# A new timetable for one core: the same 2,473 steps of a gated linear attention and an FFN, ordered anew

## The chip, the cores and the metric

One core of a Trainium2 chip runs the whole kernel. Its engines each take their own instructions in the order in which the program issues them: TensorE (PE, with the weight loads in a row of their own, PEld), VectorE (DVE), ScalarE (ACT), GpSimd (POOL), and SyncE (SP), which here only issues transfers. The metric is device time of one execution in microseconds (us); less is better.

## The reference

Two parts, one after the other. First a recurrence over 768 steps for 4 batches x 8 heads with 48 x 48 states:

```python
cur = einsum('bhd,bhe->bhde', u * k[t], v[t])
y[t] = einsum('bhd,bhde->bhe', r[t], state + cur)
state = w[t][..., None] * state + einsum('bhd,bhe->bhde', k[t], v[t])
```

Then an FFN on its output, seen as x of 3,072 tokens x 384 (8 heads x 48): `h = max(x @ w_in, 0)`, `out = (h * h) @ w_out`, with 2,048 hidden columns. `w_in` and `w_out` are 64-bit floats, everything else 32-bit. Output: 3,072 x 384 in 32 bit.

## The kernel before

**Tiling.** Time is cut into 6 chunks of 128 steps; a chunk of one batch is a unit, so there are 24 units. A chunk's four units make 512 tokens, for which the FFN runs in 16 slices of 128 hidden columns. Each slice (line 827, `ffn`) is one *first product* `hp` (9 matmuls, line 852), then `g1` (ReLU, ACT), `g2` (square; ACT in chunk 0, else DVE), `g3` (the upper part, ACT), `g4` (the rest, DVE, line 864), then four *second products* `ob`, one per batch (3 matmuls of 128 x 384 each, line 870), which add up in four PSUM banks `obs`. Products are made of upper and lower parts, which is why there are three matmuls where one would do. Six slices of chunk 0 and all 16 of chunk 1 run in two halves of two batches. Steps carry a number as their name: `hp 0` to `hp 5` are slices 0 to 5 for batches 0 and 1 of chunk 0, `hp 6` to `hp 11` the same for batches 2 and 3, `hp 12`, `hp 14`, ... the full slices, and `hp 32` is the first of chunk 1.

**Attention of a unit in chunk 0.** w, k and r arrive in time-major form and PE turns them (`turn`, line 496); DVE scans the products of w (`scan`, line 508); ACT takes logarithm and exponential (`ln`, `exp`) and copies r (`rc`, line 518); DVE multiplies (`rk` line 523, `rt`, `kn`, `kn2`, `kq`); PE makes `bp`, `mt` (scores), `mix`, `mix2` and `dS` (the new state); ACT and DVE write x as upper part and rest (`x`, line 584, `xl`, line 587). From chunk 1 on the turning is done by two DVE transposes (`z`, line 460) and 16 small transfers from SBUF to SBUF (`pt`, line 470), and PE's part is `ktp`, `dS`, `mt`, `past` and `mix` in chunk 1, `ktp` and one joint `mix` later. The state of a batch is updated by POOL (`SE`, line 680), which waits for PE's use of the old state. x of two batches is completed by small transfers (`send`, line 705).

**Weights.** Eight groups of two slices. A group g comes by five transfers for w_in (one of 384 KB, four of 96 KB; line 398) and one of 768 KB for w_out (line 400), still in 64 bit; `split_w` makes two 32-bit parts of each by ACT, three DVE steps (lines 415, 419, 424), ACT and a POOL subtraction (line 432). w, k and r come as 192 KB per batch (line 451; for two batches at once 384 KB), v as four transfers of 48 KB per unit (line 483).

**What sets the order.** All work is first recorded as 2,473 steps (`Plan.add`, with an engine, what is read and written, and buffers), numbered as they are added. `Plan.run` then issues them in the order of the table `ORDER`, takes each buffer's place from `PLACES`, and puts ahead of some PE steps the fillers that `FILLS` lists: step: (count, pool, place). A filler is a transpose of the identity into an unused place (`fill`, line 334); 16 of them run at the very start in any case. As every engine takes its instructions in order of issue, the table is the order of six queues: 593 steps on PE, 658 on ACT, 729 on DVE, 65 on POOL, 423 transfers on SP and 5 on ACT's queue. Semaphores are set from the reads and writes, whatever the order.

**Steps that the texts name by number**: 373, 380, 387, 401, 415 are `hp 0`, `hp 1`, `hp 2`, `hp 4`, `hp 6`; 781 and 788 are the first two first products of chunk 1.

Of the kernel before, what the change touches and what calls it, by code (L numbers as in the profile page):

```python
# [96 lines left out]
class Names:  # L97
# [122 lines left out]
def kernel(  # L220
# [12 lines left out]
    V, A, G, T = nc.vector, nc.scalar, nc.gpsimd, nc.tensor  # L233
# [3 lines left out]
    C = 128  # L237
# [777 lines left out]
```

## Time and profile before

| | us |
|---|---|
| median of 3 runs | 532.66 (532.25 to 536.98) |
| the profiled execution, span | 533.0 |
| PE busy | 515.3 (97%) |
| PEld, DVE, ACT, POOL busy | 464.7, 358.4, 312.6, 77.6 |
| first products, line 852: 1,062 matmuls | 220.9 busy |
| second products, line 870: 1,152 matmuls | 228.1 busy |

A busy time is the union of an engine's instructions, so it says where an engine had something in hand, not that it was of use: a filler counts as busy. The profile has 5,478 PE matmuls, which is every one of the program, so each PE step can be found in the timeline by counting. 53.07 MB pass the transfer queues in 222,982 packets, 212,672 of them under 512 bytes.

### The profile page before, as it was taken

How to read it: one execution, taken by the hardware profiler on the slowest of the kernel's cores; microseconds unless marked ns; L12 is line 12 of the kernel's file. 1: busy time of each engine (PE TensorE's matmuls, PEld its weight loads, DVE VectorE, ACT ScalarE, POOL GpSimd, SP SyncE). 2: the span in 40 equal slices, each digit the busy share in tenths (PEclk: the TensorE clock that was granted, in tenths of full speed). 3: DMA queues.
4: the chain of work that ended last, by engine and by line, in shares of the span. 5: the costliest groups of instructions: out<-in, count | busy, mean ns of one | idle time of the engine just before them, and what ended most of it. 6: DMA issues, size and time to landing. Idle time of an engine off the chain costs nothing.

```text
span 533.0 us, 13849 instructions
## 1 busy us (share of the span) xinstructions
PE 515.3 (97%) x5478; PEld 464.7 (87%) x5478; DVE 358.4 (67%) x782; ACT 312.6 (59%) x858; POOL 77.6 (15%) x117
## 2 busy tenths in 40 slices
PE   8998999999999999899999999999999999999996
PEld 8787998778899989788998988898998898989995
DVE  4899887887768799766877768648366654333332
ACT  2778888777675667757557384655345554432322
POOL 2012441242403030030300300201200000000000
PEclk9999999999999999999999999999999999999999
DMA  9999869946465655636555363543450010200001
GB/s 144 168 241 218 179 148 204 236 81 119 85 129 121 117 117 109 124 77 129 107 92 110 61 134 73 100 77 80 89 117 1 5 31 17 71 6 1 0 1 63
DMA packets 222982, 53.07 MB, mean 100 GB/s; under 512 B 212672, under 2 KB 217792, under 8 KB 222912
## 3 DMA queue, kind: packets, MB, share of 16 engines
q1 hardware_dynamic: 222192, 51.15, 48.1%
q8 instruction: 45, 0.74, 0.6%
q10 hardware_dynamic: 720, 0.98, 0.6%
q14 instruction: 25, 0.20, 0.1%
HBM read 31.65 MB, written 4.72 MB: 68 GB/s over the span
## 4 chain that ended last, share of the span: by engine, by line
PE 69%; SPq 3%; DVE 2%; DMA 2%; issue 0%; ACT 0%; POOL 0%; ACTq 0%; DVEq 0%; POOLq 0%
PE ob L870 31%; PE hp L852 30%; SPq L470 2%; PE ob L644 2%; PE ob L663 2%; PE a L653 2%; PE a L626 1%; PE hp L608 1%; DMA x<-x 1%; DVE st L460 0%; DMA pt<-st 0%; DMA v<-in_v_dram 0%; SPq L483 0%; PE hp L548 0%; DVE pt L508 0%
## 5 line engine op out<-in xcount | busy, mean ns | idle before, releaser
L870 PE MATMUL ob<-wo,g 128*128 128x384 f32 x1152 | 228.1, 341 | 2.1 <-ACT x L584 2.1
L852 PE MATMUL hp<-x,wi 128*128 128x512 f32 (+1 forms) x1062 | 220.9, 354 | 1.5 <-DVE g L864 1.3
L870 PEld LDWEIGHTS ob<-wo,g 128*128 128x128 f32 x1152 | 199.6, 188 | 9.6 <-ACT x L584 2.3
L852 PEld LDWEIGHTS hp<-x,wi 128*128 128x128 f32 x1062 | 174.6, 189 | 27.7 <-DVE g L864 4.0
L857 ACT ACTIVATE t<-hp 128x512 f32<-128x512 f32 (+1 forms) x118 | 61.0, 517 | 89.1 <-PE hp L852 53.5
L861 DVE SCALAR_TENSOR_TENSOR hp<-hp,t 128x512 f32<-128x512 f32 (+1 forms) x96 | 58.1, 605 | 78.3 <-ACT t L857 78.1
L864 DVE TENSOR_TENSOR g<-hp,g 128x512 fp32r<-128x512 f32 (+1 forms) x118 | 69.1, 586 | 39.9 <-ACT g L863 38.4
L863 ACT CAST g<-hp 128x512 fp32r<-128x512 f32 (+1 forms) x118 | 59.5, 507 | 47.0 <-DVE hp L861 46.2
L603 ACT ACTIVATE m<-diag,beta 128x64 f32<-128x64 f32 x160 | 40.3, 339 | 0.0
L508 DVE TENSOR_TENSOR_SCAN pt<-pt,zero 112x128 f32<-112x128 f32 x80 | 30.8, 420 | 7.3 <-DMA pt<-st 4.1
L634 POOL MEMSET S<- 1x1 f32 x16 | 1.4, 88 | 193.1 <-PE ob L644 192.5
L584 ACT ACTIVATE x<-ob 112x128 fp32r<-112x128 f32 x64 | 15.7, 277 | 21.0 <-PE ob L663 13.6
L557 POOL TENSOR_TENSOR st<-st 128x384 f32<-128x384 f32 x16 | 16.6, 1035 | 78.3 <-DVE st L460 53.2
L460 DVE STREAM_TRANSPOSE st<-st 128x1152 f32<-128x1152 f32 x20 | 26.9, 1360 | 0.2 <-DMA st<-in_w_dram 0.2
L587 DVE SCALAR_TENSOR_TENSOR x<-ob,x 112x128 fp32r<-112x128 f32 x64 | 16.6, 282 | 13.1 <-ACT x L584 9.3
L432 POOL TENSOR_TENSOR wi<-q,wi 128x768 fp32r<-128x768 f32 x8 | 16.2, 2026 | 50.1 <-ACT wi L431 46.5
L515 ACT ACTIVATE m<-pt 112x512 f32<-112x512 f32 x24 | 15.2, 632 | 9.0 <-DVE pt L508 8.8
L531 DVE TENSOR_TENSOR pt<-pt,m 112x512 f32<-112x512 f32 x24 | 17.2, 716 | 4.3 <-ACT Ec L530 1.9
L801 ACT COPY ob<-zero 112x128 f32<-112x128 f32 x64 | 16.3, 271 | 4.8 <-DVE x L587 3.2
L432 POOL TENSOR_TENSOR wo<-q,wo 128x768 fp32r<-128x768 f32 x8 | 14.8, 1856 | 25.0 <-ACT wo L431 22.7
L610 ACT COPY m<-hp 128x448 f32<-128x448 f32 (+1 forms) x20 | 9.9, 494 | 13.5 <-PE hp L608 13.2
L685 DVE COPY_PREDICATED m<-caus,a 128x256 f32<-128x256 uint8 x40 | 16.9, 439 | 1.1 <-PE a L653 1.0
(127 smaller groups left out, 540.1 us busy)
## 6 DMA issues: line engine op xcount, KB each, us to landing
pt<-st SPq DMA_DIRECT2D x120, 96.0 KB, 2.3
ro<-in_moe_w_out_dram SPq DMA_DIRECT2D x8, 768.0 KB, 6.6
v<-in_v_dram SPq DMA_DIRECT2D x96, 48.0 KB, 2.5
st<-in_r_dram SPq DMA_DIRECT2D x11, 384.0 KB, 5.1
st<-in_w_dram SPq DMA_DIRECT2D x11, 384.0 KB, 5.2
st<-in_k_dram SPq DMA_DIRECT2D x11, 384.0 KB, 4.6
out_dram<-q SPq DMA_DIRECT2D x20, 192.0 KB, 2.2
ri<-in_moe_w_in_dram SPq DMA_DIRECT2D x8, 384.0 KB, 5.2
```

The source lines that it names most:

```text
L432: P.add("pool", 1.9, rank(8 * k + 5), lambda q=q, tt=tt: G.tensor_tensor(out=tt[:, 1], in0=q.tile, in1=tt[:, 0].bitcast(F32), op=ALU.subtr ...
L460: V.transpose(out=zt[:, i].rearrange("a t p q i -> a t (p q) i"), in_=sv[:, :, i].rearrange("s t p q x -> s t (p q) x"))
L508: lambda p=p: V.tensor_tensor_scan(out=pt[:, 0, p], data0=src(0)[:, p], data1=zero.broadcast_to([HP, C]), initial=1.0, op0=ALU.mult, op1=A ...
L531: P.add("dve", 0.6, rank("kn"), lambda: V.tensor_tensor(out=pt[:, 0], in0=pt[:, 0], in1=yv(), op=ALU.mult), r=[y0], w=EK, port=True)
L603: A.activation(M.tile[:, o:o + Q], diag2, AF.Copy, scale=beta.tile[:, i:i + 1])
L685: P.add("dve", 0.36, rank("mask"), lambda j=j: V.copy_predicated(out=mv(j), mask=caus[:, :, 0:Q].unsqueeze(1).broadcast_to([128, 2, 2, Q]) ...
L852: T.matmul(hp.tile[:, 0:n], wi[f][:, wl, kt], xT[:, kt, xl, xs], start=(m == 0), stop=(m == 3 * KT - 1))
L857: P.add("act", 0.49 if full else 0.28, rank("g1"), lambda: A.activation(t(), h(), AF.Relu), r=[hp], w=[(g, 1)])
L861: P.add("dve", 0.605 if full else 0.337, rank("g2"), lambda: V.scalar_tensor_tensor(out=h(), in0=h(), scalar=0.0, in1=t(), op0=ALU.max, op ...
L863: P.add("act", 0.48 if full else 0.26, rank("g3"), lambda: A.copy(out=hi(), in_=h()), r=[hp], w=[(g, 0)])
L864: P.add("dve", 0.605 if full else 0.335, rank("g4"), lambda: V.tensor_tensor(out=lo(), in0=h(), in1=hi().bitcast(F32), op=ALU.subtract), r ...
L870: T.matmul(obs[b][:, 0:DM], g.tile[0][:, gl, o:o + C], wo[f][:, wl], start=(f == 0 and m == 0), stop=(f == NF - 1 and m == 2))
```

## The change

`ORDER`, `PLACES` and `FILLS` are replaced; the steps and their instructions are the same. One function changes: in `clear`, which records the four steps `zero` ahead of the joint mixes, each step now names as its predecessors the steps of chunk 0 that use the same bank of `obs`. This narrows the orders that a table may have; it adds no instruction.

```diff
 ORDER = (
-    0, 4, 11, 6, 94, 1, 14, 18, 5, 19, 20, 17, 10, 21, 8, 9, 139, 15, 7, 16, 12, 23, 2, 13, 24, 22, 25, 92, 26, 30, 27, 101,
...
+    10, 5, 0, 4, 14, 178, 18, 19, 54, 6, 1, 2, 17, 20, 26, 16, 23, 21, 15, 24, 51, 25, 22, 7, 55, 58, 9, 12, 30, 31, 33, 57, 64, 27, 60, 28, 29, 59, 11, 61,
...
 FILLS = {
-    443: (2, 'a', 1), 571: (3, 'a', 0), 363: (3, 'a', 0), 370: (4, 'hp', 1), 578: (5, 'hp', 1), 493: (3, 'hp', 0), 645: (2, 'side', 0), 511: (6, 'side', 0),
-    520: (2, 'side', 0), 634: (5, 'side', 0), 663: (4, 'hp', 0), 1215: (1, 'hp', 1), 15: (29, 'ob', 1), 30: (8, 'ob', 3), 39: (6, 'ob', 0), 80: (6, 'ob', 2),
-    89: (5, 'hp', 0), 142: (3, 'hp', 0), 124: (12, 'ob', 0), 133: (11, 'ob', 0), 162: (6, 'ob', 0),
+    14: (20, 'ob', 0), 16: (7, 'ob', 1), 55: (4, 'ob', 3), 56: (10, 'ob', 1), 71: (14, 'ob', 0), 99: (2, 'ob', 0), 41: (3, 'ob', 1), 48: (16, 'ob', 1),
+    101: (2, 'ob', 1), 82: (3, 'hp', 0), 89: (11, 'ob', 1), 156: (16, 'ob', 0), 165: (12, 'side', 0),
 }
...
     def clear(rank):
         for p in range(NP):
+            turned = [s for s in P.steps if s.name.endswith(f" of chunk 0, batch {s.name[-1]}") and ("ob", p) in s.keys]
-            P.add("act", 0.16, rank("zero"), lambda p=p: A.copy(out=obs[p][0:HP, DM:], in_=zero[0:HP].broadcast_to([HP, C])), w=[("YO", p)], banks=1 << p)
+            P.add("act", 0.16, rank("zero"), lambda p=p: A.copy(out=obs[p][0:HP, DM:], in_=zero[0:HP].broadcast_to([HP, C])), w=[("YO", p)], after=turned, banks=1 << p)
```

Read with the steps' names, PE's queue begins like this (c0b2: chunk 0, batch 2; a number in brackets: so many fillers ahead of the step):

```
before: ut, turn c0b0, [29] turn c0b0, turn c0b0, [8] bp c0b0, turn c0b2, turn c0b1, turn c0b1, turn c0b1, mt c0b0, [6] mix c0b0,
 turn c0b2, bp c0b1, mix2 c0b0, mt c0b1, turn c0b3, dS c0b0, [6] mix c0b1, mix2 c0b1, turn c0b2, [5] dS c0b1, [3] turn c0b3, hp 0,
 bp c0b2, turn c0b3, hp 1, bp c0b3, mt c0b2, [12] mix c0b2, mix2 c0b2, [11] dS c0b2, [6] mt c0b3, ob 0, hp 2, hp 3, mix c0b3, ob 0, ob 1, ...
after: [20] turn c0b0, ut, [7] turn c0b0, turn c0b0, [4] turn c0b1, bp c0b0, turn c0b1, [10] turn c0b1, [14] bp c0b1, mt c0b0,
 [2] turn c0b2, turn c0b3, mt c0b1, mix c0b0, [3] mix2 c0b0, turn c0b2, [16] dS c0b0, [2] turn c0b2, mix c0b1, [3] mix2 c0b1, bp c0b2,
 [11] dS c0b1, hp 0, turn c0b3, hp 1, turn c0b3, [16] bp c0b3, mt c0b2, hp 2, mix c0b2, ob 0, mix2 c0b2, ob 0, hp 3, ob 1, ...
```

and in chunk 1's attention, from its 72nd step on, like this:

```
before: hp 16, [3] bp c1b1, ob 12, ob 12, bp c1b0, hp 18, [3] ktp c1b0, ob 12, ob 12, dS c1b0, [4] mt c1b0, [5] past c1b0, ob 14, mix c1b0, ...
after: hp 16, bp c1b0, ob 12, ob 14, ob 12, ob 12, hp 18, ob 14, ob 14, ob 12, ktp c1b0, ob 16, ob 16, bp c1b1, dS c1b0, ob 16, ob 14, mt c1b0, ...
```

SP's queue begins before with w, a quarter of v, r (batch 0), r (batches 2 and 3), k (batch 0); after with a quarter of v, k, w (batch 0), 96 KB of weights 0, a quarter of v (batch 1), r (batch 0).

## Rows read from the trace of the kernel before

**Rows 1.** The page: busy time by engine, clock by slice, one costly group.
```profile
PE 515.3 (97%) x5478; PEld 464.7 (87%) x5478; DVE 358.4 (67%) x782; ACT 312.6 (59%) x858; POOL 77.6 (15%) x117
...
PEclk9999999999999999999999999999999999999999
...
L801 ACT COPY ob<-zero 112x128 f32<-112x128 f32 x64 | 16.3, 271 | 4.8 <-DVE x L587 3.2
```

**Rows 2.** Windows by stage: us, busy us (count) by engine, clock, DMA share, GB/s.
```profile
0.00:33.00 33.00, 28.98 (x361) 25.72 (x362) 22.99 (x62) 17.70 (x52) 4.40 (x21) 1.00 1.01 173
33.00:60.99 27.99, 25.79 (x342) 23.32 (x340) 25.94 (x42) 23.04 (x64) 7.86 (x5) 1.00 0.89 213
60.99:140.00 79.01, 75.53 (x770) 65.58 (x771) 66.27 (x113) 64.01 (x156) 26.19 (x17) 1.00 0.73 152
140.00:220.00 80.00, 76.95 (x1032) 72.48 (x1032) 61.85 (x171) 53.33 (x179) 13.09 (x21) 1.00 0.60 115
220.00:528.40 308.40, 308.05 (x2981) 277.60 (x2979) 180.83 (x395) 154.47 (x410) 26.04 (x55) 1.00 0.32 64
528.40:533.00 4.60, 0.00 (x0) 0.00 (x0) 0.56 (x1) 0.00 (x0) 0.00 (x0) 0.87 0.28 97
```

**Rows 3.** The same windows, fillers' line L334 alone: PE and PEld busy, clock, DMA.
```profile
0.00:33.00 33.00, 12.37 (x73) 10.97 (x73) 1.00 1.01 173
33.00:60.99 27.99, 3.83 (x29) 3.12 (x29) 1.00 0.89 213
60.99:140.00 79.01, 6.27 (x39) 4.62 (x39) 1.00 0.73 152
```

**Rows 4.** Timeline of DVE, to 60 us.
```profile
13.03 0.69 DVE L523 TENSOR_TENSOR m<-pt,ob 112x512 f32<-112x512 f32 x1 [4.57 <-ACT pt L518]
...
55.60 0.38 DVE L864 TENSOR_TENSOR g<-hp,g 128x256 fp32r<-128x256 f32 x1
...
58.14 0.42 DVE L587 SCALAR_TENSOR_TENSOR x<-a,x 128x256 fp32r<-128x256 f32 x1
58.48 0.95 DVE L419 SCALAR_TENSOR_TENSOR q<-ro,q 128x768 uint32<-128x768 uint32 x1
```

**Rows 5.** Timeline of SP's queue, to 112 us: start and us of an issue.
```profile
4.26 2.27 SPq L451 DMA_DIRECT2D st<-in_k_dram  x1
...
50.56 2.48 SPq L398 DMA_DIRECT2D ri<-in_moe_w_in_dram  x5
57.41 2.77 SPq L470 DMA_DIRECT2D pt<-st  x4
...
95.88 1.98 SPq L483 DMA_DIRECT2D v<-in_v_dram  x1
```

**Rows 6.** Windows: the stretch in which DVE is full.
```profile
13.03:58.56 45.53, 41.02 (x583) 36.27 (x581) 41.65 (x77) 35.83 (x105) 9.45 (x5) 1.00 0.94 209
```

**Rows 7.** Timeline of POOL, 60 to 140 us.
```profile
94.54 0.75 POOL L680 TENSOR_TENSOR S<-S,Ec 112x192 f32<-112x192 f32 x1 [12.01 <-PE a L644]
95.26 1.83 POOL L432 TENSOR_TENSOR wi<-q,wi 128x768 fp32r<-128x768 f32 x1
```

**Rows 8.** Timeline of PE: start, us, what, idle before it with releaser.
```profile
1.60 3.68 PE L334 MATMUL a<-ident 128*128 128x128 f32 x16 [1.60 <-POOL ident masks.py:199]
...
6.85 4.65 PE L334 MATMUL ob<-ident 128*128 128x128 f32 x29
...
38.61 1.53 PE L334 MATMUL ob<-ident 128*128 128x128 f32 x12
...
48.93 2.31 PE L852 MATMUL hp<-x,wi 128*128 128x256 f32 x18
...
60.99 2.41 PE L852 MATMUL hp<-x,wi 128*128 128x256 f32 x18
...
218.74 0.79 PE L870 MATMUL ob<-wo,g 128*128 128x384 f32 x3 [2.08 <-ACT x L584]
```

**Rows 9.** Chain of waits, end of the span: start, us, what.
```profile
521.52 6.87 PE ob L870 x39
```

190 rows, old and new, of tables (ORDER, PLACES) are left out of this document.

## The prediction

> **What bounds the kernel now.** I read the page first: TensorE (PE) is busy 97% of the span and its granted clock is in the top tenth in every slice, so PE's own queue is the path [rows 1]. How much of it is not product work? The windows by stage give the idle time: 4.02 us up to 33, 2.20 up to 60.99 (where the first product of the third and fourth batch starts), 3.48 up to 140 (the first products of chunk 1), 3.05 up to 220, 0.35 in the 308 us after that, and a tail of 4.60 after the last product [rows 2]. Busy hides a second loss: the fillers, transposes of the identity that only keep PE running. The same windows for their line alone give 12.37, 3.83 and 6.27 us; a single one stands later [rows 3]. Idle and fillers together are 40.2 us of 533.0: 16.4, 6.0, 9.8, 3.05, 0.35 and 4.6 by stage. After 220 there is nothing for an order to win. All that can move is in the first 220 us.
>
> Why PE waits there, in order. Up to 13 us: VectorE (DVE) sits 4.57 us until the turned r of the first batch is copied; the k that is turned just ahead of it is the fifth transfer of the SP queue, and its issue alone took 2.27 us at 4.26, behind a load of r for two other batches [rows 4, 5]. From 13.03 to 58.56, where DVE ends the last rest (line 587) of batch 3, DVE is busy 41.65 of 45.53 us [rows 6]: here PE's fillers stand beside a full DVE. From 61 on DVE has air (66.27 of 79.01) [rows 2], and PE waits for things that stand in a queue: GpSimd (POOL) waited 12.01 us for a PE result with the update of the state, and the subtraction for weights 5 queued behind it began the moment that was over, at 95.26 [rows 7]. SP's v transfer at 95.88 is one for chunk 2 that has to wait for PE, and weights 6 and 7 stand behind it [rows 5].
>
> **The change, stage by stage.** No instruction of a step is added or removed; queues and fillers are new. Counts below are from the tables.
>
> *Fillers: 126 become 120* (the 16 at the start stay). 12 in 1.53 us is 128 ns each, 29 in 4.65 is 160 [rows 8]: six fewer are worth 0.8 to 1.0 us. Where they stand matters more: 92 instead of 57 ahead of the first product (373), 28 instead of 29 from there to 415, and none instead of 40 after it.
>
> *0 to 60.99 (product 415).* PE floor: busy less fillers in the two stages is 28.98 + 25.79 - 12.37 - 3.83 = 38.6 us, fillers 16.2 for 102; 34 more by 128 ns are 4.4; with the start's 1.6, and the dS of batch 3 (0.6) now behind 415, that is 38.6 + 20.6 + 1.6 - 0.6 = 60.2 [rows 2, 3, 8]. DVE floor: w of batch 0 is now third on SP instead of first, and 20 fillers by 160 ns stand ahead of its turning, so the first scans end near 10.9 instead of 8.46 (13.03 less the 4.57 of idle); but k is second, so the product r*k (13.03 now) can start near 12.0: turning at 5.3 + 3.2 = 8.5, then 7 fillers (0.9) and a small product, two turns and the copy, by estimate 2.6 together (each of such steps is near the 0.69 of the multiplication's row). From there DVE has the same work as before up to that last rest plus three steps (two splits at 0.95, one g4 at 0.38) [rows 4]: 12.0 + 45.5 + 2.3 = 59.8, and 415 starts 2.4 us behind it as now, at 62.2. If DVE's 3.9 us of idle shrink, PE's floor of 60.2 holds. I take 61.9: **+1.0**, ends -0.8 and +4.5 (the 35 additional fillers ahead of 373, all unhidden).
>
> *60.99 to 140.* Removed: 6.27 us of fillers. Do the waits that they filled come back? In the order of before, successive PE steps of a unit of chunk 1 (ktp, dS, mt, past, mix) have 2, 0, 0, 1 other PE steps between them for batch 0 and 2, 0, 2, 0 for batch 2; in the new one 3, 2, 4, 2 and 2, 2, 2, 1, nowhere none. A second product takes 0.53 us (three matmuls of the 39 in 6.87 us) [rows 9], as long as three or four fillers at 6.27 us for 39 [rows 3], and the groups of fillers taken out there had two to six: the gaps are covered by real work. That work has to be there: weights 5 to 7. In POOL's queue the subtractions of weights 5, 6 and 7 (wi) now stand ahead of the state update that held them; the v of chunk 2 goes from place 103 of SP to 189; the last piece of weights 5's wi goes from place 91 to 81, of weights 6 from 98 to 93. So I count the fillers as gone and 1.2 of 3.48 us of idle time with them: **-7.5**. Cover: DVE would do its 66.27 us in 71.5, 93%, as tight as 13 to 58.6 is now; if that fails the gain is the DVE's to withhold. Ends: 0 (each filler becomes a wait) and -9.8.
>
> *140 to 220.* 2.1 of 3.05 us is one wait of a second product for the evacuation of x on ScalarE [rows 8]. The queues around it are all new; the PE distance is not. I take **-1.5**, ends 0 and -3.3. *After 220* and *tail*: 0; the last evacuation moves from DVE to ScalarE, of like length. *The four zero steps* of chunk 2 (0.27 us each [rows 1]) come forward by 95 to 200 places; ScalarE is busy 64.01 of 79.01 us at the tightest [rows 2], so one early copy costs its 0.27 at most, which is inside the +1.0. The new dependency of `clear` adds no instruction.
>
> Sum on the profiled execution: 533.0 + 1.0 - 7.5 - 1.5 = 525.0. The median of the runs shown is 532.66, 0.37 below that execution, so **524.7 us**. By the ends: 533.0 - 0.8 - 9.8 - 3.3 = 519.1 less 0.4, and a little more if stretched products inside "busy" tighten too.
>
> **Rivals.** 1 per cent, 5.3 us, is about what a measurement of this kernel can tell from no change.
>
> *A, forecast*: 516 to 529, chance 0.62 (0.04 of it above 527.3).
>
> *B, the waits come back.* DVE and ScalarE, not order, set the pace of 61 to 140; fillers turn into idle time. For it: DVE at 93% needed. Against: POOL and SP rows show a queue, not a busy engine, ending the waits. 533.0 + 1.0 - 2 - 1 = 531, 530.6 as a run. Chance 0.16.
>
> *C, slower: SP's queue blocks at its 52nd place.* There the new order has the first transfer that waits for the transposes of chunk 1; SP holds everything behind it. Now that wait comes at place 60 and already costs SP the time from 53.04 (50.56 and 2.48) to 57.41 [rows 5]. Eight transfers that are now issued before it fall behind it: 96 KB x 3 and 768 KB of weights 4 and four v of 48 KB, 1,248 KB, at the 213 GB/s of that stage 5.9 us [rows 2]. It decides if the transfer engines run dry, that is if the transposes end later than what is queued lands; with DVE's work ahead of them unchanged (near 57) and fewer bytes queued that is likely for some of it. It costs only if weights 5 to 7 then come later, since 61 to 140 has a DMA share of 0.73 and could catch up. If it all lands on the path: gain of the second stage gone, 533.0 + 1.0 + 5.9 = 539.9, 539.5 as a run. Chance 0.10.
>
> *D, slower: the clock.* The granted clock is 1.00 in every stage with products although PE idles up to 4.02 us in one [rows 2], with fillers in the gaps. With none in chunk 1, PE could fall to the lower level, 1.2 GHz, where product work takes twice as long: 15 us of it there would give 525 + 15 = 540. Against: gaps get second products. The Trainium skill ("TensorE: Matmul & The Clock Gate", Part 1) has the half rate as the default state that only activity lifts, which speaks against taking 40 fillers out; by that rule stage two would be the one to lose, and no row here shows the fall while products run. Chance 0.03.
>
> *E, it doesn't do what it says.* The description has few fillers ahead of the first products; the table has 92 ahead of the first FFN product and 55 instead of 37 ahead of the first scores. If those hold the queue with nothing won back up to 415: 533.0 + 4.5 - 7.5 - 1.5 = 528.5, 528.1 as a run. Chance 0.09.
>
> **How the numbers follow.** Likeliest is A: 524.7. Range 516 to 535: A, B and E whole; outside are C, D and some 0.07 of A below 516. Faster by over 1% (under 527.3): A's 0.58. Within 1%: B, E and the rest of A, 0.29. Slower: C and D, 0.13.
>
> **What would show it.** First FFN product near 34 to 36 us instead of 33, product 387 near 42 to 44 instead of 48.93 [rows 8], and 415 between 60 and 63. The fillers' row for 61 to 140 empty and PE's idle time there under 3.5 us; POOL's subtraction for weights 5 before its first state update. The first products of chunk 1 (781) near 130 to 134 instead of just under 140. Wrong, if idle time in 61 to 140 exceeds 8 us (B), if SP shows a gap over 8 us ahead of the first pt transfer and the weights 5 come after 96 (C), if a granted clock under 1 shows (D), or if 415 comes after 64 (E).

## The result: 0.7% slower, and the profile after

| | kernel before | changed kernel |
|---|---|---|
| median of 20 runs each, us | 535.24 (532.25 to 539.21) | 538.59 (535.88 to 541.65) |
| ratio, 95% interval | | 1.0073 (1.0051 to 1.0096) |
| the profiled execution, span | 533.0 | 534.2 |

Forecast was 524.7, with a range of 516 to 535. The ratio excludes both "faster" and "no change", but stays inside the 1% that the three chances called "within".

The page of the changed kernel: busy time, the granted clock in 40 slices, and the shares of engines on the chain that ended last.

```profile
PE 514.2 (96%) x5472; PEld 463.8 (87%) x5472; DVE 361.1 (68%) x782; ACT 314.3 (59%) x858; POOL 78.6 (15%) x117
...
PEclk9999998998999999999999999999999999999998
...
PE 70%; SPq 14%; DMA 6%; DVE 5%; issue 2%; ACT 2%; POOL 0%; DVEq 0%; ACTq 0%; POOLq 0%
```

Three eights stand in the clock line that had none [rows 1]: in the slices that begin at 80 and at 120 us, and in the last one, most of which lies behind the last product. SP's queue is 14% of the chain, where the page of the kernel before has 3%. The windows by stage, at the bounds of [rows 2], place it:

```profile
0.00:33.00 33.00, 30.99 (x399) 28.09 (x400) 24.89 (x66) 19.71 (x59) 5.82 (x22) 1.00 1.09 190
33.00:60.99 27.99, 27.99 (x372) 26.00 (x363) 24.72 (x43) 25.56 (x66) 9.44 (x5) 1.00 0.88 195
60.99:140.00 79.01, 70.60 (x707) 60.38 (x706) 60.53 (x106) 60.14 (x151) 21.98 (x13) 0.96 0.71 150
140.00:220.00 80.00, 77.86 (x1138) 73.75 (x1140) 67.88 (x182) 55.04 (x180) 15.18 (x25) 1.00 0.60 114
220.00:528.40 308.40, 306.25 (x2884) 275.39 (x2876) 183.03 (x390) 153.42 (x405) 26.14 (x54) 1.00 0.32 64
```

The same windows for the fillers' line alone:

```profile
0.00:33.00 33.00, 15.99 (x108) 13.91 (x108) 1.00 1.09 190
33.00:60.99 27.99, 3.44 (x28) 3.07 (x28) 1.00 0.88 195
60.99:140.00 79.01, 0.00 (x0) 0.00 (x0) 0.96 0.71 150
```

From 61 to 140 the fillers are gone, 6.27 to 0, and the idle time is 8.41 us where it was 3.48. The clock there is 0.96, where it was 1.00. The trace's record of the clock has two stretches at the lower of the two levels, 1.2 GHz: 80.9 to 84.3 and 128.7 to 132.1 us. What TensorE did around both (start, us, instruction, in brackets the idle time before it and what ended it):

```profile
39.91 1.34 PE L864 MATMUL hp<-x,wi 128*128 128x256 f32 x9
...
57.08 1.23 PE L864 MATMUL hp<-x,wi 128*128 128x256 f32 x9
...
75.50 2.34 PE L864 MATMUL hp<-x,wi 128*128 128x512 f32 x9 [1.58 <-DVE g L876]
77.68 1.22 PE L882 MATMUL ob<-wo,g 128*128 128x384 f32 x6
81.11 3.82 PE L864 MATMUL hp<-x,wi 128*128 128x512 f32 x9 [2.20 <-DVE g L876]
...
125.70 1.05 PE L559 MATMUL hp<-ut,m 112*128 112x4 f32 x8 [2.25 <-DVE m L534]
...
128.87 3.82 PE L864 MATMUL hp<-x,wi 128*128 128x512 f32 x9
...
139.79 2.42 PE L864 MATMUL hp<-x,wi 128*128 128x256 f32 x18
```

`hp 6` starts at 57.08, 3.9 us ahead of before (60.99 [rows 8]). Then `hp 14` waits 1.58, `hp 16` waits 2.20 and takes 3.82 us instead of 2.34, and the lead is gone. The same nine matmuls take 3.82 again at 128.87. 781 starts at 139.79, where it was 138.63.

Both waits were ended by a g4 on VectorE. VectorE's timeline in the changed kernel, with idle time before an instruction in brackets:

```profile
72.57 0.56 DVE L426 TENSOR_SCALAR q<-q 128x768 uint32<-128x768 uint32 x1 [1.75 <-ACT q L422]
73.16 0.96 DVE L430 SCALAR_TENSOR_TENSOR q<-ro,q 128x768 uint32<-128x768 uint32 x1
74.16 0.96 DVE L435 SCALAR_TENSOR_TENSOR q<-ro,q 128x768 uint32<-128x768 uint32 x1
75.03 0.42 DVE L876 TENSOR_TENSOR g<-hp,g 128x256 fp32r<-128x256 f32 x1
79.42 1.06 DVE L519 TENSOR_TENSOR_SCAN pt<-pt,zero 112x128 f32<-112x128 f32 x3 [3.97 <-DMA pt<-st]
80.39 0.67 DVE L876 TENSOR_TENSOR g<-hp,g 128x512 fp32r<-128x512 f32 x1
...
123.86 1.78 DVE L534 TENSOR_TENSOR m<-pt 112x512 f32<-112x512 f32 x1 [1.62 <-DMA pt<-st]
```

VectorE was not full. It stood 3.97 us for a transfer, with the g4 that TensorE needed queued behind the scans; g4 at 11 stood behind three splits that had waited for weights 3. The transfers' side is SP's queue (start, us of issuing):

```profile
65.58 0.65 SPq L411 DMA_DIRECT2D ro<-in_moe_w_out_dram  x1
66.27 2.09 SPq L481 DMA_DIRECT2D pt<-st  x3
68.41 2.72 SPq L494 DMA_DIRECT2D v<-in_v_dram  x1
...
74.21 1.97 SPq L481 DMA_DIRECT2D pt<-st  x3
...
98.55 0.40 SPq L411 DMA_DIRECT2D ro<-in_moe_w_out_dram  x1
106.65 3.79 SPq L481 DMA_DIRECT2D pt<-st  x4
```

From 53 to 99 us SP issues one transfer after another with one gap, of 0.45 us; most take 0.4 to 0.7 us each, a few 2 or more. The Trainium skill ("Perfetto Trace Analysis", What "DMA-bound" means) counts an issuing sequencer whose track is solid as a limit of its own, beside the DMA engines. This stretch is solid in that sense, but its rows do not part the issues from the DMA engines, whose mean share in the stage is 0.71. The `ro` at 65.58 (weights 3) landed at 71.56, pt20, the last of the three at 74.21, at 79.20.

### The profile page after: what moved, and what is told of

It reads as the page before. It is cut to its first block, busy times and chain, and to the rows that moved or that the text cites. A ratio compares the mean times of both kernels' runs of the same rounds, so it can differ in the third digit from the quotient of the medians.

```text
span 534.2 us, 13846 instructions
## 1 busy us (share of the span) xinstructions
PE 514.2 (96%) x5472; PEld 463.8 (87%) x5472; DVE 361.1 (68%) x782; ACT 314.3 (59%) x858; POOL 78.6 (15%) x117
## 4 chain that ended last, share of the span: by engine, by line
PE 70%; SPq 14%; DMA 6%; DVE 5%; issue 2%; ACT 2%; POOL 0%; DVEq 0%; ACTq 0%; POOLq 0%
PE ob L882 29%; PE hp L864 29%; SPq L481 6%; SPq L494 4%; SPq L409 2%; DMA ro<-in_moe_w_out_dram 2%; PE ob L655 2%; DMA pt<-st 2%; PE ob L674 1%; PE a L664 1%; PE ob L345 1%; DMA st<-in_k_dram 1%; SPq L462 1%; PE a L637 1%; PE hp L619 1%
## 5 line engine op out<-in xcount | busy, mean ns | idle before, releaser
L864 PE MATMUL hp<-x,wi 128*128 128x512 f32 (+1 forms) x1062 | 223.8, 357 | 7.3 <-DVE g L876 5.8
L519 DVE TENSOR_TENSOR_SCAN pt<-pt,zero 112x128 f32<-112x128 f32 x80 | 32.2, 440 | 8.1 <-DMA pt<-st 7.2
L542 DVE TENSOR_TENSOR pt<-pt,m 112x512 f32<-112x512 f32 x24 | 18.3, 764 | 3.0 <-ACT m L527 2.2
L570 POOL TENSOR_TENSOR st<-st,un 128x384 f32<-128x384 f32 x16 | 16.5, 1038 | 0.8
```

Of the source, the lines that this page charges most:

```text
L519: lambda p=p: V.tensor_tensor_scan(out=pt[:, 0, p], data0=src(0)[:, p], data1=zero.broadcast_to([HP, C]), initial=1.0, op0=ALU.mult, op1=A ...
L864: T.matmul(hp.tile[:, 0:n], wi[f][:, wl, kt], xT[:, kt, xl, xs], start=(m == 0), stop=(m == 3 * KT - 1))
```

## Experiments

Three theories were set against each other. **Cover**: the fillers in chunk 1 had stood in waits that are there anyway. **Clock**: TensorE, with waits and no fillers, falls to the lower level. **Queue order**: g4 waits behind VectorE instructions that wait for transfers. Step numbers are the tables'. The columns behind the ratio are read from one profiled execution of each kernel. "hp 0 to the last ob" is the time from the start of the first first product to the start of the last second product of the profiled run; it leaves out the start, where `hp 0` came between 33.0 and 35.3 us in different runs.

| run | ratio to before, 95% | hp 6 | hp 16 | 781 | hp 0 to the last ob | half clock, 57 to 144 us |
|---|---|---|---|---|---|---|
| before | | 60.99 | 80.66 | 138.63 | 494.7 | none |
| changed | 1.0073 (1.0051, 1.0096) | 57.08 | 81.11 | 139.79 | 495.1 | 3.4 + 3.4 |
| fills in waits | 0.9987 (0.9963, 1.0011) | 58.65 | 83.51 | 138.69 | 490.9 | none |
| g4 before scans | 1.0024 (0.9998, 1.0051) | 57.83 | 78.91 | 139.21 | 493.1 | 3.4 + 10.2 |
| before, no fillers from 61 | 0.9997 (0.9968, 1.0026) | 61.74 | 81.42 | 142.43 | 495.1 | 6.8 |
| new start, old rest | 1.0172 (1.0139, 1.0204) | 58.33 | 86.91 | 151.85 | 503.8 | 6.8 + 6.8 + 6.8 |
| old start, new rest | 1.0059 (1.0024, 1.0094) | 61.16 | 85.05 | 142.76 | 496.6 | 6.8 |
| g4 and fills | 0.9892 (0.9843, 0.9940) | 57.77 | 79.67 | 136.80 | 487.7 | none |
| and weights 7 early | 0.9899 (0.9846, 0.9953) | 58.64 | 80.14 | 137.05 | 488.2 | none |
| and kn later | 0.9878 (0.9828, 0.9928) | 58.32 | 80.11 | 135.05 | 486.2 | none |
| and g4 before bh | 0.9876 (0.9844, 0.9909) | 59.24 | 80.81 | 136.76 | 486.3 | none |
| kn later, no fill at bp | 0.9895 (0.9863, 0.9926) | 58.11 | 79.88 | 134.63 | 485.5 | none |
| kn later, no fill at 73 | 0.9890 (0.9860, 0.9921) | 58.90 | 80.13 | 137.10 | 487.6 | 3.4 |

One execution says little about 1 or 2 us: "before" and "before, no fillers from 61" have the same order and the same single filler behind 781, and from there to the last ob they take 389.1 and 386.4. Nor does the last column tell all. In the run with g4 before bh the clock was also at half from 19.5 to 22.9 us, and the kernel before, at 1.00 up to its last product in its profile, is not always so. The mean granted clock is on record for each execution; 1 less that clock, times the span, is an estimate of the time given up to the lower level:

| kernel | executions | mean clock | given up, us |
|---|---|---|---|
| before | 29 | 0.9957 (0.991 to 1.000) | 2.3 |
| changed | 20 | 0.9876 (0.981 to 0.995) | 6.7 |
| fills in waits | 12 | 0.9968 | 1.7 |
| g4 before scans | 11 | 0.9886 | 6.1 |
| before, no fillers from 61 | 11 | 0.9918 | 4.4 |
| g4 and fills | 6 | 0.9985 | 0.8 |
| and kn later | 6 | 0.9970 | 1.6 |
| kn later, no fill at bp | 6 | 0.9952 | 2.6 |
| kn later, no fill at 73 | 6 | 0.9965 | 1.9 |

Some of it falls behind the last product and costs nothing (0.6 us in the profile of before, 1.4 in that of the changed kernel). The changed kernel gives up 4.4 us more than the one before, and the medians differ by 3.35: over many executions the clock can account for the whole loss.

**Fills in the waits.**

```diff
 FILLS = {
+    466: (18, 'a', 0), 475: (28, 'a', 0), 634: (28, 'hp', 1),
```

> The changed kernel with 74 short transposes in three of its waits: 18 ahead of hp at 14, 28 ahead of hp at 16 (both into a PSUM tile that is free there), 28 ahead of bp of chunk 1, batch 2. Queues and places as in the changed kernel. Clock theory (TensorE fell to half clock at 80.9 and 128.7 us for 3.4 us each because it had just stood idle; hp at 16 took 3.8 instead of 2.2 us, hp at 30 as well): both stretches go, the waits stay as long as they were, 3.2 us less than the changed kernel, ratio to the kernel before about 1.001. Rival (the clock falls for another reason, or falls elsewhere instead): a stretch at half clock remains, ratio 1.005 to 1.008.

Its window from 61 to 140 and three steps of TensorE:

```profile
60.99:140.00 79.01, 77.44 (x802) 68.95 (x801) 63.25 (x109) 62.09 (x154) 23.44 (x14) 1.00 0.74 155
```

```profile
80.53 3.22 PE L347 MATMUL a<-ident 128*128 128x128 f32 x28
83.51 2.31 PE L866 MATMUL hp<-x,wi 128*128 128x512 f32 x9
85.66 0.95 PE L561 MATMUL hp<-ut,m 112*128 112x4 f32 x8
```

Clock 1.00, `hp 16` back to 2.31 us, and 0.86% less than the changed kernel: 74 useless transposes make it faster. hp 0 to the last ob falls by 4.2 us. Of these, 2.7 come up to 781, where the two `hp` at half clock had cost 3.0 (2 x 1.5); 1.6 lie behind 781 (386.9 us from there to the last ob instead of 388.5), which no theory had named.

**g4 ahead of the scans.** VectorE's steps alone:

```diff
 ORDER = (
-    244, 245, 246, 454, 348, 349, 346, 461, 347,
+    244, 245, 454, 246, 461, 348, 349, 346, 347,
```

> The changed kernel with four steps of VectorE's queue in another order: g4 at 12 ahead of the three scans of chunk 1, batch 0, that wait for pt20 (landed at 79.20 us), and g4 at 11 ahead of the last split of weights 3. Queue-order theory (TensorE waited at 73.9 and 78.9 us because g4 stood behind VectorE instructions that waited for transfers): hp at 14 starts near 74.6 instead of 75.50, hp at 16 near 78.9 instead of 81.11, the half clock at 81 goes with the wait; 2 to 4 us less than the changed kernel, ratio 0.999 to 1.004. Transfer theory (the transfers of chunk 1 are late whatever stands behind them): the same wait comes back before bp of chunk 1, batch 0 or at hp at 18, ratio 1.005 to 1.008.

```profile
60.99:140.00 79.01, 74.70 (x716) 65.07 (x715) 59.07 (x108) 61.30 (x152) 21.93 (x13) 0.91 0.72 153
```

```profile
74.71 2.34 PE L865 MATMUL hp<-x,wi 128*128 128x512 f32 x9
...
78.91 2.33 PE L865 MATMUL hp<-x,wi 128*128 128x512 f32 x9 [0.80 <-DVE g L877]
```

Both starts came where the queue-order theory had them, 74.71 and 78.91. But the half clock did not go with the wait: it came at 84.5 instead, and a second stretch, from 122.0, lasted 10.2 us. This kernel idles less than the changed one (4.31 us in this window, 8.41 there) and spends more time at the lower level. Over all its executions the mean clock is no better than the changed kernel's, 0.9886 beside 0.9876. So the clock is not simply the price of those two waits.

**The kernel before without its 39 fillers from 61 on.** The eleven entries 443, 571, 363, 370, 578, 493, 645, 511, 520, 634, 663 leave `FILLS`.

> The kernel before, without the 39 short transposes that it had between 61 and 140 us (its filler row there: 6.27 us with their waits); all else as before. Cover theory (they stood in waits that are there anyway): waits take their place, clock stays 1.00, ratio 0.998 to 1.002. My prediction's term (they were time on TensorE that a gap does not give back): 3 to 6 us faster, ratio 0.989 to 0.995. Clock theory: one or two stretches at half clock appear, 1.6 us each, ratio 1.003 to 1.006.

```profile
60.99:140.00 79.01, 71.37 (x681) 61.24 (x684) 63.51 (x112) 62.48 (x150) 22.66 (x13) 0.96 0.72 152
```

This is the prediction's biggest term by itself, and it is nothing: 0.9997. Idle time goes from 3.48 to 7.64 us and 6.8 us pass at half clock. What the fillers took, waits and clock take back. Over the executions the clock falls from 0.9957 to 0.9918, 2.1 us more given up by the estimate above, and the time stays: the fillers did cost time, and the clock that they held was worth as much.

**Two splices at `hp 6`.** First 285 steps of one order (284 in the second splice), then all others in the order of the other:

```python
head = ORDER_new[:285]
ORDER = head + [n for n in ORDER_old if n not in head]
```

> The first 285 steps of the changed kernel's order (up to hp at 6, which starts at 57.1 instead of 61.0 us), all later steps in the order of the kernel before, with its fillers; buffer places dealt anew where the old ones clash. If the 3.9 us gained by hp at 6 can be kept by a better order behind it: ratio about 0.993. Transfer theory (weights 3 and the pt transfers, issued one after another by SP from 53 us on, land no earlier, so TensorE waits for them): the lead is gone by hp at 16, ratio 0.998 to 1.002. If the clock theory holds too and waits come without fillers, up to 1.005.

```profile
64.92 2.65 SPq L497 DMA_DIRECT2D v<-in_v_dram  x4
67.68 3.06 SPq L484 DMA_DIRECT2D pt<-st  x4
70.79 0.64 SPq L497 DMA_DIRECT2D v<-in_v_dram  x1
71.49 1.30 SPq L484 DMA_DIRECT2D pt<-st  x2
72.83 0.64 SPq L414 DMA_DIRECT2D ro<-in_moe_w_out_dram  x1
```

```profile
81.85 4.18 PE L867 MATMUL hp<-x,wi 128*128 128x512 f32 x9 [5.49 <-DVE g L879]
```

A miss, and not a test of the lead. The splice puts five v and six pt on SP ahead of weights 3, whose `ro` is issued at 72.83 instead of 65.58; `hp 14` stands 5.49 us and starts at 81.85 instead of 75.50. It shows how hard SP's order bites: 7.3 us more of issuing ahead of one transfer come out as 6.4 us on TensorE.

> The other splice: the first 284 steps of the order of before (up to hp at 6, at 61 us), all later steps as in the changed kernel, without fillers from there on. Waiting theory (the 3.9 us that the changed kernel is ahead at hp at 6 are waited away by hp at 16, where transfers of SP's queue land): hp at 16 at 81 to 83 us all the same, ratio to before 1.005 to 1.010, like the changed kernel. Additive theory (each stage keeps its own length): hp at 16 near 85, ratio about 1.0145. The first splice showed that a seam can put weights 3 behind other transfers of SP; a gap over 4 us at hp at 14 would be that.

```profile
85.05 2.25 PE L865 MATMUL hp<-x,wi 128*128 128x512 f32 x9
```

Half of each theory. `hp 16` is 3.9 us later, as the additive one has it, so the lead is not yet absorbed there; but hp 0 to the last ob is only 1.5 us more than in the changed kernel and the two ratios can't be told apart. Of the 4.0 us by which `hp 16` is later, counted from hp 0, 1.0 is gone at 781 and 1.5 more behind it. `bp` of chunk 1, batch 2 stands 0.41 us here and 2.25 there, but the `bp` after it stands 1.58 us here; where the 2.5 us went is not shown.

**Order and fills together, then three single moves.**

```diff
 FILLS = {
+    466: (4, 'a', 0), 475: (12, 'a', 0), 358: (6, 'a', 0), 634: (28, 'hp', 1),
```

> The run with g4 ahead of the scans, with 50 short transposes more: 4 ahead of hp at 14, 12 ahead of hp at 16, 6 ahead of bp of chunk 1, batch 0, 28 ahead of bp of chunk 1, batch 2. Without them it had 13.6 us at half clock (84.5 to 87.9, 122.0 to 132.3), and its groups of matmuls took 6.8 us longer there than at the full clock. Clock theory: full clock to the end, 4 to 6.5 us less than that run, ratio to before 0.991 to 0.995. Rival (what the clock gives back is waited for at the next transfer): ratio 0.997 to 1.002 at a full clock.

```profile
60.99:140.00 79.01, 76.44 (x784) 67.43 (x783) 64.61 (x112) 62.40 (x157) 25.27 (x16) 1.00 0.75 156
```

At the full clock, 1.3% less than the run with g4 alone and 1.1% less than the kernel before. Whether this is the new timetable's gain is not shown: the kernel before with two g4 moved and other fills was not run.

```diff
 # SP alone; weights 7's w_out is step 308
-    290, 604, 603, 614, 610, 308,
+    290, 308, 604, 603, 614, 610,
```

> The run before it, with one transfer moved on SP's queue: load 1 of weights 7 (issued at 110.5 us between the pt transfers of chunk 1, batch 2, landed at 116.2) issued in SP's idle time at 99 us; 24 instead of 28 transposes ahead of bp of chunk 1, batch 2. Queue theory (each issue holds SP about 0.65 us, and split 8 of weights 7 stands in ScalarE's queue ahead of the copies that mix of chunk 1, batch 1 needs): the wait of 0.4 to 0.9 us before that mix goes, pt10 lands 0.65 us earlier, 1 to 1.5 us less than the run before it. Rival: nothing, since DMA engines and VectorE set these times: within 0.3 us.

No gain shows, as the rival had it: 0.9899 beside 0.9892, with intervals too wide for 1 us, and 488.2 us from hp 0 to the last ob beside 487.7. The wait before that mix had already gone with the change of timing in the run before.

```diff
 # VectorE alone
-    568, 367, 366, 369, 368,
+    367, 366, 369, 368, 568,
```

> The run before it, with kn of chunk 1, batch 1 (2.3 us on VectorE, 93.8 to 96.1) behind the four sums S and S2 of chunk 1, batch 0, instead of ahead of them. mt of chunk 1, batch 0 waited 1.1 us for these sums. Queue theory: mt starts 1 us earlier, 0.5 to 1 us less than the run before it. Rival: kn is late instead and ktp of chunk 1, batch 1 waits for it: no change or up to 1 us more.

Counted from hp 0, 781 comes 0.9 us earlier and the last ob 2.0 us; `mt` no longer waits, as the queue theory had it. The ratio, 0.9878, agrees but can't be told from 0.9899. Its windows:

```profile
60.99:140.00 79.01, 77.35 (x791) 68.28 (x790) 65.76 (x118) 64.72 (x162) 25.52 (x16) 1.00 0.75 157
140.00:220.00 80.00, 79.99 (x1178) 76.52 (x1179) 68.23 (x189) 57.46 (x189) 11.32 (x21) 1.00 0.64 124
```

```diff
 # VectorE alone
-    746, 747, 785,
+    746, 785, 747,
```

> The run with kn later (the fastest so far), with one more step of VectorE moved: bh of chunk 2, batch 0 (1.7 us) behind g4 at 32 instead of ahead of it. hp at 34 stood 1.0 us for that g4 in the kernel changed and in every run since. Queue theory: the 1.0 us goes, ratio to the run with kn later 0.998. Rival: diag of chunk 2, which needs bh, is late instead: no change.

```profile
140.58 1.23 PE L866 MATMUL hp<-x,wi 128*128 128x256 f32 x9
```

The wait before `hp 34` went, as the queue theory had it, but hp 0 to the last ob stayed (486.3 beside 486.2). Something behind it took the 1.0 us; what it was stays open.

**Which fills are needed?** Taken out of the run with kn later: `634`, then `466`, `475` and `358`.

> The run with kn later, without its 24 short transposes ahead of bp of chunk 1, batch 2. In that run rk, for which this bp waited 2.3 us in the changed kernel, is done at 119.5 us, before TensorE comes to the transposes at 120.4, so they cost 2.4 us and fill no wait. If TensorE keeps its clock: 2.4 us less than the run with kn later, ratio to before about 0.983. Clock theory in the form that it wants no long wait: this one, as there is no wait. Rival (the clock wants more work than this stretch has, waits or not): a stretch of 3.4 to 6.8 us at half clock between 120 and 135 us, 1.7 to 3.4 us back, ratio 0.986 to 0.990.

> The run with kn later, without its 22 short transposes between 73 and 83 us; the 24 ahead of bp of chunk 1, batch 2 stay. The waits there are 0.4 us at hp at 14, 1.0 at hp at 16, 0.3 at bp of chunk 1, batch 0. If the transposes hold the clock here too: 3.4 us at half clock near 84 as in the run with g4 ahead of the scans, 1.5 to 2.5 us more than the run with kn later, ratio 0.990 to 0.993. Rival: no fall, ratio 0.986 to 0.988.

Windows of these two, the first without 24 at `bp`, the second without 22 from 73 to 83:

```profile
60.99:140.00 79.01, 75.55 (x768) 65.78 (x767) 65.92 (x118) 64.41 (x161) 25.60 (x16) 1.00 0.75 157
```

```profile
60.99:140.00 79.01, 76.35 (x768) 67.10 (x766) 64.08 (x113) 63.51 (x159) 24.64 (x16) 0.98 0.72 156
```

One wait of each, in the same order:

```profile
123.94 1.05 PE L561 MATMUL hp<-ut,m 112*128 112x4 f32 x8 [1.05 <-ACT beta L567]
```

```profile
83.68 1.05 PE L560 MATMUL hp<-ut,m 112*128 112x4 f32 x8 [1.21 <-DVE g L877]
```

Without the 24 this execution shows no fall, and 0.6 us less, not 2.4, since the next `bp` then stood 1.05 us. Without the 22, 3.4 us at half clock come at 85.2, and hp 0 to the last ob is 1.4 us more. But these are single executions. The three ratios overlap, and the mean clocks of six executions each, 0.9970 with all fills, 0.9952 without the 24 and 0.9965 without the 22, do not bear out that the 22 are needed and the 24 are not. Which of them are needed stays open.

## Why the prediction was wrong

**0 to 60.99: +1.0 forecast, -3.9 came.** Wrong in sign. `hp 2` came at 39.91 (42 to 44 forecast). The first rk came at 10.69 (12.0 forecast). From it to the last rest of batch 3 VectorE took 46.1 us (56.77 less 10.69), not 47.8. And 415 followed 0.3 us behind instead of 2.4: in the kernel before it had waited for g4 at 4, which came only at 60.94, while here g4 was done at 56.44. My 2.4 us was another wait in the old order, not a length. The fillers were mis-costed too: 102 of them at 16.2 and 34 more, 20.6 us, were forecast; 136 took 19.4, 15.99 and 3.44.

**60.99 to 140: -7.5 forecast, +5.1 came** (`hp 6` to 781: 77.64 before, 82.71 after). This is the step that failed, in the words "So I count the fillers as gone". Taken out alone, the fillers are worth 0.9997. The step counted a filler as time on TensorE that neither a wait nor the clock takes back; both did. Idle time rose from 3.48 to 8.41 us, and two first products ran at half clock, 3.0 us more. I had asked whether TensorE steps stand between two steps of a unit, and they do; but 6.0 of the 8.4 us of waits are not between those. They stand at first products, for a g4 queued behind VectorE instructions that wait for a transfer, and at `bp` for a rk that waits for one. Two more came between steps of a unit all the same, at `mt` and `mix` (a row of waits: what waited, for whom, us in total, times, longest):

```profile
PE a L664 <- DVE S L687: 1.1, 1, 1.1
PE a L674 <- ACT nothing L833: 0.9, 1, 0.9
```

The trace of the kernel before had the signs. What TensorE still waited for in that stage, besides its fillers, was work on VectorE and ScalarE, g4 and rk among it, and neither POOL nor SP, which the prediction named:

```profile
115.85 2.33 PE L852 MATMUL hp<-x,wi 128*128 128x512 f32 x9 [0.51 <-DVE g L864]
125.21 1.05 PE L548 MATMUL hp<-ut,m 112*128 112x4 f32 x8 [0.73 <-DVE m L523]
```

The prediction counted distances on TensorE's queue and busy time on VectorE (93% needed, 60.53 of 79.01 used), and never followed VectorE's own queue against landing times. POOL's part was right and worth little: the subtraction for weights 5 now comes at 93.58, ahead of the state update, and waits for ScalarE instead [rows 7]. Rival C took SP's stretch for a question of bytes; the trace shows a row of issues.

**140 to 220: -1.5 forecast, about -0.9 came** (TensorE's idle time in that window, 3.05 to 2.14). The 2.08 us wait for x did go; two waits of first products for a g4 came, 0.85 and 1.19 us. Behind 220, where I had put 0, idle time rose from 0.35 to 2.15 us, 1.25 of it a first product's wait for a transfer of x. From 781 to the last ob it is -0.6 in all.

**The base.** I took the median of three executions, 532.66, as 0.37 us below the profiled one. Twenty give 535.24, and in every execution with both on record the time is 1.6 to 2.1 us above the span: the 0.37 was no step from span to time, and 524.7 stood some 2 us too low before any stage was wrong.

**The rivals.** B's sign came (idle above 8 us: 8.41), and so did D's (clock 0.96). C's queue has a part in it, but not at the point it gave: SP's gap ahead of the first pt is 4.8 us (48.27 to 53.03), not over 8; what harm there is lies behind it, where the queue is full. E is out by its own sign, `hp 6` came at 57. I gave B 0.16 and D 0.03; the truth is both together, with A's early lead in a place where I had forecast a loss. For D, I wrote that gaps get second products. The rule I cited for it, that only activity lifts TensorE from the half rate (the Trainium skill, "TensorE: Matmul & The Clock Gate", Part 1), spoke for what came, a clock of 0.96 in that stage without fillers and 1.00 with them; I weighed "no row here shows the fall" as evidence against, when the rows came from a kernel with fillers in eleven places of that stage.

**The account, changed against before.** In the two profiled executions: `hp 0` to `hp 6` -4.1; two `hp` at half clock +3.0; the rest of the way to 781 +2.1, a remainder, in which new waits outweigh the fillers that are gone; 781 to the last ob -0.6: +0.4 us in all (495.1 less 494.7). With `hp 0` 0.15 later and 0.6 more behind the last ob, the span is 1.1 us longer. The medians differ by 3.35, so this pair of executions holds only a third of the loss; the mean clocks, 0.9876 and 0.9957, are what the record has for the rest. Shown by runs: the fills give the clock back and 0.86%; the two g4 moves give 0.5%; both give 1.8%, and then the kernel is 1.1% ahead of the one before.

**What stays open.** What makes the clock fall. The changed kernel fell once in the last 0.2 us of a wait of 2.20 us, and once 3.0 us behind the end of one of 2.25. The run without the 22 fills fell with none longer than 1.21, the one without the 24 did not fall with one of 1.05, and the kernel before kept 1.00 at a wait of 2.08 [rows 8]. The longest idle time alone does not sort these, and in other executions of the kernel before the mean clock went down to 0.991. Whether the 1.1% could be had in another way than with fills, by steps of TensorE moved into these places, or on the old timetable, was not tried.

## What to carry to other kernels

A filler in a tuned kernel has two prices: the time it takes and the clock it holds; test its removal alone before counting it as a gain. When an order is made by a timetable, check each in-order queue for instructions that wait for transfers with short, urgent work behind them: two g4 of 0.4 and 0.7 us, moved ahead of a split and of the scans, were worth 2.2 us at `hp 16`. A lead won early need not last: of 4.0 us at `hp 16`, 1.5 were left at the last product. And where the clock differs from execution to execution, look at the mean clock of many before a single profile is believed.

## What the hardware showed unexpectedly

TensorE stayed at half clock while it was busy: in the run with g4 ahead of the scans the clock fell at 122.0, in the last 0.3 us of a wait of 2.25 us, and stayed low for 10.2 us, of which TensorE was busy 9.95. The stretches lasted 3.4, 6.8 or 10.2 us, nine matmuls of 512 columns took 3.82 us in them and 2.24 to 2.34 outside. And SP's queue is a serial resource by its issues: mostly 0.4 to 0.7 us each, for 48 KB (a v: 0.64) as for 768 KB (a `ro`: 0.65 and 0.40), so that the five v ahead of a `ro` in the first splice held SP for 3.3 us.
